# Thirty-two-byte gaps between the activation buffers of an fp32r feed-forward kernel

## The chip, the cores and the metric

The kernel runs on one core of a Trainium2 chip. The metric is the time of one execution on the device in microseconds (us), as the median over runs. TensorE multiplies: it loads a stationary operand of 128 columns (LDWEIGHTS, PEld in the profile) and streams a moving operand of up to 512 columns through it (MATMUL, PE). Both operands lie in the on-chip buffer memory as 128 partitions of consecutive bytes; the result goes to the accumulators. VectorE (DVE), ScalarE (ACT) and GpSimd (POOL) do elementwise work, SyncE (SP) issues the transfers.

## What is computed

Attention over a local window with block summaries, then a feed-forward layer with a squared relu. Cut to what matters:

```python
# q, k, v: (4, 8, 768, 64); x: (3072, 512); w_in: (512, 2048); w_out: (2048, 512)
scores = [scale * q @ k.T within |i - j| < 16, scale * q @ blockmax(k).T + log(32)]
a = softmax(scores)
x = a @ [v, blockmean(v)]          # heads side by side: 3072 rows of 512
h = x @ w_in
g = s * relu(h) ** 2 + b
out = g @ w_out
```

## The kernel before

The 3,072 rows are taken in twelve chunks `c` of 256. For each chunk the attended values `x` (four tiles of 128 features by 256 rows) are made, then sixteen steps `f`, each for 128 of the 2,048 hidden features. Nearly all matmuls of the feed-forward part are done in fp32r, one quick pass, so each operand is split into an upper part (rounded to fp32r) and a lower part (what is left), and a product takes three matmuls: lower weights with upper x, upper weights with lower x, upper with upper.

- `hidden` (L431 to L446) makes `ph`, 128 features by 256 rows. For each of the three terms and each of four pieces `kc`, the stationary operand is a piece of the weights (`wl_in` or `wh`, 128 columns of 512 bytes) and the moving one a piece of `xh` or `xl` (256 columns, 1,024 bytes). That is twelve matmuls a step, at L444.
- `activate` (relu, then square), `scaled` (L460, times s plus b, on POOL) and `split_rows` (L468, on DVE) make `gh` and `gl`, 1,024 bytes a partition each.
- `project` (L476 to L491) accumulates into two tiles `po`. Here the roles are swapped: the stationary operand is half of `gl` or `gh` (128 columns, 512 bytes), the moving one a row of weights (`wh` or `wl_out`, 512 columns, 2,048 bytes). For each of the two halves `t` come gl with wh, gh with wl_out, gh with wh: six matmuls a step, at L488.

The eight steps of chunk 0 that are not in THREE (f below 8) use plain fp32: one tile `g0` in a place of the ring of `gh`, and each matmul is issued as two passes. The other eight steps of chunk 0 read copies `x0h` and `x0l` of the attended values, which lie in slots of the weights.

Order: chunks 0 and 1 follow a list written by hand (FIRST_ORDER). From chunk 2 on, blocks of four steps alternate: 48 matmuls of `hidden` for four steps, then 24 of `project` for the four steps before them, with transposes (`pt`), scores (`ps`) and attended values (`pav`) of the next chunk between the blocks. Each engine runs its instructions in that order, and waits by semaphores for what it reads and for the last reader of a buffer that it overwrites.

Buffers: pools are laid out one after another in each partition in the order in which they are opened, and within a pool the tiles by first use, each rounded up to 32 bytes. `slots` (16 tiles of 4,096 bytes: raw weights, then the pairs `wh` of in and out) starts at byte 4,864, `wring` (33 tiles of 2,048 bytes, `wl_in`, `wl_out` and the plain weights `wf`) at 70,400, `stage` at 137,984, `p2` at 150,272, `p3` (tiles `qk` and `vw`) at 208,832. In `p2`: two `xh` of 4,096 bytes from 171,968; two `r`; eight `gh` of 1,024 from 182,208; two `xl` of 4,096 from 190,400; two `g`; seven `gl` of 1,024 from 200,640. The tile sizes of weights, x and g are multiples of 512.

Of the kernel before, what the change touches and what calls it, by code (L numbers as in the profile page):

```python
# [11 lines left out]
F32 = mybir.dt.float32  # L12
F32R = mybir.dt.float32r
# [6 lines left out]
P = 128  # L20
# [9 lines left out]
T = NSUB * SUB  # L30
# [4 lines left out]
NKC = DM // P  # L35
# [9 lines left out]
def windowed_attention_then_relu2_ffn(ctx, tc, qk, vwin, kt, vt, kq, vrow, wp, out):  # L45
# [6 lines left out]
    wring = ctx.enter_context(tc.tile_pool(name="wring", bufs=2 * NF + 1))  # L52
    stage = ctx.enter_context(tc.tile_pool(name="stage", bufs=4))
    p2 = ctx.enter_context(tc.tile_pool(name="p2", bufs=2))
    p3 = ctx.enter_context(tc.tile_pool(name="p3", bufs=3))
    ps_po = ctx.enter_context(tc.tile_pool(name="ps_po", bufs=2, space=bass.MemoryType.PSUM))
    ps_h = ctx.enter_context(tc.tile_pool(name="ps_h", bufs=2, space=bass.MemoryType.PSUM))
    ps_s = ctx.enter_context(tc.tile_pool(name="ps_s", bufs=2, space=bass.MemoryType.PSUM))
# [50 lines left out]
    def steps(c):  # L109
        return SECOND if c == 1 else tuple(range(NF))  # L110
# [32 lines left out]
    def whole(key):  # L143
        uses[key] += 1
        return w_f[key] if uses[key] < (2 if key[1] in THREE else 3) else w_f.pop(key)
# [80 lines left out]
    def copy(by_dve, out_, in_):  # L226
        if by_dve:
            nc.vector.tensor_copy(out_, in_)
        else:
            nc.scalar.copy(out_, in_)  # L230
# [11 lines left out]
    qk_t, vw_t, ps_of, pr_of, mn_of, sm_of, pt_of, pT_of, o_of, xt, xl = ({} for _ in range(11))  # L242
# [153 lines left out]
    def attended_part(c, p):  # L396
        kcs = slice(p, p + (1 if c < 2 else 2))
        return kcs, o_of[c, p][:, : (kcs.stop - p) * T].rearrange("p (k t) -> p k t", t=T)

    def attended(c, p, other=False):  # L400
        if p == 0:
            xt[c] = p2.tile([P, NKC, T], F32R if c else F32, name="xh", tag="xh")
        kcs, o = attended_part(c, p)
        copy(other, xt[c][:, kcs], o)

# [53 lines left out]

    def scaled(c, f, other=False):  # L460
        if c == 0 and f not in THREE:
            g = p2.tile([P, T], F32, name="g0", tag="gh", bufs=8)
        else:
            g = p2.tile([P, T], F32, name="g")
        gg[c, f] = (g,)
        (nc.vector if other else nc.gpsimd).tensor_scalar(g, r_of.pop((c, f)), s_col, b_col, ALU.mult, ALU.add)  # L466

    def split_rows(c, f):  # L468
        (g,) = gg[c, f]
        gh = p2.tile([P, T], F32R, name="gh", tag="gh", bufs=8)  # L470
        nc.vector.tensor_copy(gh, g)  # L471
        gl = p2.tile([P, T], F32R, name="gl", bufs=7)
        nc.vector.tensor_tensor(gl, g, gh.bitcast(F32), ALU.subtract)  # L473
        gg[c, f] = gh, gl

    def project(c, f):  # L476
        if f == steps(c)[0]:
            for t in range(T // P):
                po[t] = ps_po.tile([P, DM], F32, name="po", tag="po")
        g = gg.pop((c, f))  # L480
        if c == 0 and f not in THREE:
            terms = [(g[0], whole(("out", f)))]
        else:
            gh, gl = g
            terms = [(gl, w_h["out", f]), (gh, w_l["out", f]), (gh, w_h["out", f])]
        for t in range(T // P):
            for n, (a, w) in enumerate(terms):
                nc.tensor.matmul(  # L488
                    po[t], a[:, t * P : (t + 1) * P], w,
                    start=(f == steps(c)[0] and n == 0), stop=(f == steps(c)[-1] and n == len(terms) - 1),  # L490
                )  # L491

    def evict(c, t, other=False):
        o = stage.tile([P, DM], F32, name="o", tag="stage")
        copy(other, o, po[t])
        bi, ci = place(c)
        r0 = bi * S + ci * T + t * P
        nc.sync.dma_start(out[r0 : r0 + P, :], o)
# [37 lines left out]
    def of(fn, s):  # L536
# [5 lines left out]
        "W": keep_warm, "K": k_max, "k": fill_k, "Z": scores_of_maxima, "S": scores, "M": masked, "E": exps,  # L542
        "N": normalize, "T": transposes, "C": turned, "V": values, "U": values_of_means, "R": mean_of_rows,
        "L": load_k, "F": mean_done, "t": fill_v, "X": attended, "y": attended_low, "Xh": first_upper, "Xl": first_lower,
        "Ai": of(scale_weights, "in"), "Ao": of(scale_weights, "out"), "Bi": of(convert_weights, "in"),
        "Bo": of(convert_weights, "out"), "D": lambda f: convert_weights(("in", f), ("out", f)),
        "Y": hidden_part, "H": hidden, "J": activate, "G": scaled, "g": split_rows, "P": project, "O": evict,
        "hi": of(upper_weights, "in"), "ho": of(upper_weights, "out"), "li": of(lower_weights, "in"),
        "lo": of(lower_weights, "out"),
# [22 lines left out]
    for c in range(2, NC):  # L572
        bi, ci = place(c)
        for p in range(NPAIR):
            base, v_at = NF * (c - 1) - 1, (9, 10, 4, 5)[p]
            tr = 8 + 4 * (p // 2)
            lags = (1, 1, 1, 2, (12, 13, 11, 11)[p], tr, tr, 16, 17)
            m, e0, e1, n, fv, tr, tu, va, xa = (base + lag for lag in lags)
            if ci == 0:
                then(base - 12 + p, LOAD, load_k, bi, p)  # L580
                then(base - 7 + p, ATT, k_max, bi, p)
                if p < 2:
                    for third in range(3):
                        then(base + v_at - 5 + third, LOAD, load_v, bi, p, third)
                        then(base + v_at - 1 + third // 2, ATT, v_sum, bi, p, third)
                    then(base + v_at + 1, ATT, v_mean, bi, p)
            then(base - 6, LOAD, load_unit, c, p)
            then(base + v_at, LOAD, load_values, c, p)
            then(base - 2, ATT, fill_k, c, p)
            for j in range(2):  # L590
                then(base, VISIT, scores, c, p, j)
                then(m, NEXT if p < 2 else ATT, masked, c, p, j)
                then((e0, e1)[j], NEXT if p < 2 else ATT, exps, c, p, j)
            then(n, ATT, normalize, c, p)
            then(fv, ATT, fill_v, c, p)
            then(tr, PE_ATT, transposes, c, p)
            then(tu, CHAIN, turned, c, p)
            then(va, VISIT, values, c, p)
            if p % 2 == 0:
                then(xa, ATT, attended, c, p)  # L600
                then(xa, ATT, attended_low, c, p)
# [4 lines left out]
    for i in range(NF, NC * NF):  # L606
        c, j = divmod(i, NF)
        f = steps(c)[j]

        then(i - i % 4, HID, hidden, c, f)  # L610
        for stage_of in (activate, scaled, split_rows):
            then(i, CHAIN, stage_of, c, f)
        then((i + 4) | 3, PROJ, project, c, f)
        if j == NF - 1:
            for t in range(T // P):
                then((i + 4) | 3, EVICT, evict, c, t)
# [60 lines left out]
```

## Time and profile before

| what | us |
|---|---|
| median of 2 runs (631.05 to 631.11) | 631.08 |
| the profiled execution | 630.93 |
| its span, first to last instruction | 629.2 |
| TensorE matmul busy | 616.5 |
| TensorE weight load busy | 550.7 |
| VectorE, ScalarE, GpSimd busy | 328.3, 308.7, 187.7 |

The busy time of PE is a union of spans that overlap, since a matmul starts before the one ahead of it has left the array. So the pace of matmuls is read from start to start, or from a whole block of them in the chain that ended last. PEclk in the profile is the clock that TensorE was granted, in tenths of full speed. In rows of groups the numbers behind the bar are busy us, mean ns of one, idle us of the engine just ahead of them. In rows of waits the numbers are us in total, times, and the longest in us.

### The profile page before, as it was taken

To read this page: it belongs to the slowest core of one execution; us is meant where nothing else is said; L and a number is where in the kernel's file an instruction comes from. 1 tells how busy PE (TensorE), PEld (TensorE's weight loads), DVE (VectorE), ACT (ScalarE), POOL (GpSimd) and SP (SyncE) were. 2 spreads that over 40 slices of the span, in tenths; PEclk is the share of its full clock that TensorE was granted. 3 is DMA by queue.
4 is the path that set the end of the run, shared out by engine and by line. 5 is a ranking of instruction groups with operands and counts; after the bars stand their busy time and mean duration, and the time that the engine had idled before them with its cause. 6 is when DMAs were issued, how large, how long until landed. Compare 5 with 4: busy or idle time off the path is not lost.

```text
span 629.2 us, 14328 instructions
## 1 busy us (share of the span) xinstructions
PE 616.5 (98%) x5330; PEld 550.7 (88%) x5330; DVE 328.3 (52%) x1092; ACT 308.7 (49%) x939; POOL 187.7 (30%) x351
## 2 busy tenths in 40 slices
PE   6999999999999999999999999999999999999997
PEld 5757878989989998999899999998998999899896
DVE  6999899865354246345454335336435324523311
ACT  4999975453463364265245426436345336323321
POOL 3126442211511422322242331341151151232211
PEclk9999999999999999999999999999999999999999
DMA  8999503006205015203502211600710500200000
GB/s 333 413 416 416 222 26 126 17 2 190 79 18 181 1 44 200 74 19 102 165 20 87 94 44 38 236 19 1 218 62 7 181 0 19 85 2 1 34 1 33
DMA packets 26997, 66.45 MB, mean 106 GB/s; under 512 B 3824, under 2 KB 3824, under 8 KB 26928
## 3 DMA queue, kind: packets, MB, share of 16 engines
q1 hardware_dynamic: 26928, 65.54, 29.3%
q8 instruction: 42, 0.69, 0.5%
q14 instruction: 27, 0.22, 0.1%
HBM read 59.09 MB, written 6.29 MB: 104 GB/s over the span
## 4 chain that ended last, share of the span: by engine, by line
PE 87%; DVE 4%; ACT 2%; issue 1%; POOL 1%; DVEq 0%; POOLq 0%; ACTq 0%
PE po L488 40%; PE ph L444 38%; PE pav L394 3%; PE pt L358 3%; PE ps L308 3%; DVE wf_out L141 1%; POOL g L466 1%; DVE wl_in L155 1%; DVE wf_in L141 0%; DVE wf_in L139 0%; ACT r L458 0%; DVE wf_out L139 0%; ACT wraw L125 0%; ACT wraw L126 0%; ACT r L452 0%
## 5 line engine op out<-in xcount | busy, mean ns | idle before, releaser
L466 POOL TENSOR_SCALAR g<-r,sb_col 128x256 f32<-128x256 f32 x189 | 127.1, 673 | 379.2 <-ACT r L458 256.0
L471 DVE CAST gh<-g 128x256 fp32r<-128x256 f32 x184 | 54.9, 298 | 244.0 <-POOL g L466 244.0
L452 ACT ACTIVATE r<-ph 128x256 f32<-128x256 f32 x179 | 67.6, 378 | 206.1 <-PE ph L444 187.0
L488 PE MATMUL po<-wh,gl 128*128 128x512 f32 x368 | 146.3, 397 | 0.0
L488 PE MATMUL po<-wh,gh 128*128 128x512 f32 x368 | 145.0, 394 | 0.0
L488 PE MATMUL po<-wl_out,gh 128*128 128x512 f32 x368 | 144.2, 392 | 0.0
L444 PE MATMUL ph<-xh,wl_in 128*128 128x256 f32 x704 | 109.9, 278 | 0.1
L444 PE MATMUL ph<-xl,wh 128*128 128x256 f32 x704 | 108.8, 276 | 0.0
L444 PE MATMUL ph<-xh,wh 128*128 128x256 f32 x704 | 108.7, 276 | 0.0
L473 DVE TENSOR_TENSOR gl<-g,gh 128x256 fp32r<-128x256 f32 x184 | 85.8, 466 | 33.6 <-PE po L488 16.4
L444 PEld LDWEIGHTS ph<-xh,wl_in 128*128 128x128 f32 x704 | 96.8, 188 | 4.8 <-issue 0.5
L444 PEld LDWEIGHTS ph<-xl,wh 128*128 128x128 f32 x704 | 93.6, 188 | 0.0
L444 PEld LDWEIGHTS ph<-xh,wh 128*128 128x128 f32 x704 | 93.0, 188 | 0.0
L339 ACT ACTIVATE pr<-pr,mn 128x120 f32<-128x120 f32 x176 | 67.0, 382 | 38.6 <-DVE mn L326 38.4
L458 ACT ACTIVATE r<-r 128x256 f32<-128x256 f32 x184 | 77.0, 418 | 15.2 <-DVE r L454 9.7
L488 PEld LDWEIGHTS po<-wh,gl 128*128 128x128 f32 x368 | 69.1, 188 | 14.8 <-issue 1.4
L488 PEld LDWEIGHTS po<-wh,gh 128*128 128x128 f32 x368 | 69.2, 188 | 14.3
L488 PEld LDWEIGHTS po<-wl_out,gh 128*128 128x128 f32 x368 | 69.2, 188 | 13.8
L270 POOL COPY vw<-vsum 24x256 f32<-24x256 f32 x88 | 41.7, 503 | 20.9 <-DMA vsum<-vmean 9.5
L230 ACT COPY o<-po 128x512 f32<-128x512 f32 x24 | 14.0, 589 | 42.3 <-PE po L488 41.3
L339 ACT ACTIVATION_READ_ACCUMULATOR pr<-pr,mn 128x1 f32 x176 | 33.0, 187 | 0.0
L349 DVE TENSOR_TENSOR pr<-pr,rs 128x480 f32<-128x480 f32 x48 | 32.0, 666 | 1.7
(90 smaller groups left out, 565.4 us busy)
## 6 DMA issues: line engine op xcount, KB each, us to landing
wraw<-in_wp_dram SPq DMA_DIRECT2D x32, 512.0 KB
qk<-in_qk_dram SPq DMA_DIRECT2D x44, 369.0 KB
vw<-in_vwin_dram SPq DMA_DIRECT2D x48, 256.0 KB
out_dram<-o SPq DMA_DIRECT2D x24, 256.0 KB
kraw<-in_kt_dram SPq DMA_DIRECT2D x12, 384.0 KB
vraw<-in_vt_dram SPq DMA_DIRECT2D x12, 252.0 KB
kq<-in_kq_dram SPq DMA_DIRECT2D x4, 512.0 KB
vraw<-in_vt_dram SPq DMA_DIRECT2D x6, 264.0 KB
```

The source lines that it names most:

```text
L270: nc.gpsimd.tensor_copy(vw_t[c, p][WIN:KR, e], vsum[bi][WIN : WIN + NB, 2 * p + e, :].unsqueeze(1).to_broadcast([NB, NSUB, D]),)
L308: nc.tensor.matmul(o, qi, kw[r, i, :], start=True, stop=True)
L339: nc.scalar.activation(pr, pr, AF.Exp, bias=mn_of[c, p][:, n : n + 1], scale=-1.0, accum_out=sm_of[c, p][:, n : n + 1])
L349: nc.vector.tensor_tensor(pr, pr, rs.unsqueeze(2).to_broadcast([P, 4, KR]), ALU.mult)
L358: nc.tensor.transpose(pt_of[c, p][:KR, n * P : (n + 1) * P], pr[:, n, :], ident)
L444: nc.tensor.matmul(ph, w[:, kc * P : (kc + 1) * P], x[:, kc], start=(n == 0), stop=(n == len(terms) - 1))
L452: nc.scalar.activation(r, ph, AF.Relu)
L458: nc.scalar.activation(r, r, AF.Square)
L466: (nc.vector if other else nc.gpsimd).tensor_scalar(g, r_of.pop((c, f)), s_col, b_col, ALU.mult, ALU.add)
L471: nc.vector.tensor_copy(gh, g)
L473: nc.vector.tensor_tensor(gl, g, gh.bitcast(F32), ALU.subtract)
L488: nc.tensor.matmul(po[t], a[:, t * P : (t + 1) * P], w, start=(f == steps(c)[0] and n == 0), stop=(f == steps(c)[-1] and n == len(terms) - 1),
```

## The change

The rings of `xh` (two), `gh` (eight) and `gl` (seven) leave the pool `p2`. Each of their buffers becomes a tile of its own in one of three new pools `px`, `pg` and `pl`, opened behind `p2`, and a tile of 32 bytes that nothing uses is put ahead of a buffer where GAP, LGAP or XGAP say so. `apart` hands out the buffers from a list; `project` gives a step's buffers back when it has issued its matmuls.

```diff
+    px, pg, pl = (ctx.enter_context(tc.tile_pool(name=n, bufs=1)) for n in ("px", "pg", "pl"))
+    XGAP, GAP, LGAP = (0, 32), (0,) + (32,) * 7, (0,) + (32,) * 5 + (0,)
+    free, made = {"xh": [0, 1], "gh": list(range(8)), "gl": list(range(7))}, set()
+    places = {}
+
+    def apart(pool, name, shape, dtype, gaps):
+        if free[name]:
+            n = free[name].pop(0)
+        else:
+            n = next(o[name] for o in places.values() if name in o)
+            next(o for o in places.values() if name in o).pop(name)
+        if (name, n) not in made and gaps[n]:
+            pool.tile([P, gaps[n] // 4], F32, name=f"gap_{name}_{n}")
+        made.add((name, n))
+        return n, pool.tile(shape, dtype, name=name, tag=f"{name}{n}", bufs=1)
...
-            xt[c] = p2.tile([P, NKC, T], F32R if c else F32, name="xh", tag="xh")
+            n, xt[c] = apart(px, "xh", [P, NKC, T], F32R if c else F32, XGAP)
+            free["xh"].append(n)
...
-            g = p2.tile([P, T], F32, name="g0", tag="gh", bufs=8)
+            n, g = apart(pg, "gh", [P, T], F32, GAP)
+            places[c, f] = {"gh": n}
...
-        gh = p2.tile([P, T], F32R, name="gh", tag="gh", bufs=8)
+        nh, gh = apart(pg, "gh", [P, T], F32R, GAP)
         nc.vector.tensor_copy(gh, g)
-        gl = p2.tile([P, T], F32R, name="gl", bufs=7)
+        nl, gl = apart(pl, "gl", [P, T], F32R, LGAP)
+        places[c, f] = {"gh": nh, "gl": nl}
...
+        for name, n in places.pop((c, f)).items():
+            free[name].append(n)
```

By the sizes above, `xh` then lies at 185,280 and 189,408, `gh` at 193,504 and on in steps of 1,056 bytes, `gl` at 201,920 and on in steps of 1,056 (the last in one of 1,024), `xl` at 174,016, and `p3` starts 416 bytes later, at 209,248. The weights stay where they are.

## The prediction

> **What bounds the kernel now.** I read the page first: busy times, granted clock, the chain's shares by engine and line, and the costliest groups.
>
> ```profile
> span 629.2 us, 14328 instructions
> ...
> PE 616.5 (98%) x5330; PEld 550.7 (88%) x5330; DVE 328.3 (52%) x1092; ACT 308.7 (49%) x939; POOL 187.7 (30%) x351
> ...
> PEclk9999999999999999999999999999999999999999
> ...
> PE 87%; DVE 4%; ACT 2%; issue 1%; POOL 1%; DVEq 0%; POOLq 0%; ACTq 0%
> ...
> L488 PE MATMUL po<-wh,gl 128*128 128x512 f32 x368 | 146.3, 397 | 0.0
> L488 PE MATMUL po<-wh,gh 128*128 128x512 f32 x368 | 145.0, 394 | 0.0
> L488 PE MATMUL po<-wl_out,gh 128*128 128x512 f32 x368 | 144.2, 392 | 0.0
> ```
>
> TensorE is busy for 98% of the span at full clock, holds 87% of the chain, and has no idle time ahead of these groups. So the end moves only if matmuls follow each other at another pace. The mean durations (392 to 397 ns) overlap, so the pace has to come from start to start. The chain in order of time gives it by whole blocks, start and length in us:
>
> ```profile
> 131.05 5.66 PE ph L444 x48
> ...
> 346.31 0.87 PE pt L358 x8
> ...
> 598.20 5.47 PE ph L444 x48
> 603.67 5.49 PE po L488 x24
> 609.16 5.47 PE ph L444 x48
> 614.63 11.00 PE po L488 x48
> ```
>
> A block of 24 projection matmuls takes 5.49 us, 228.8 ns each; a block of 48 hidden ones 5.47 us, 114.0 ns each; 8 transposes 0.87 us, 108.8 ns each. One early ph block took 5.66 us instead of 5.47. The timeline (start, length in us) shows single starts; a merged row "x4" is left for the next one by four matmuls:
>
> ```profile
> 347.96 0.39 PE L488 MATMUL po<-wl_out,gh 128*128 128x512 f32 x1
> ...
> 350.02 0.39 PE L488 MATMUL po<-wl_out,gh 128*128 128x512 f32 x1
> ```
> ```profile
> 353.46 0.62 PE L444 MATMUL ph<-xh,wh 128*128 128x256 f32 x4
> ...
> 357.54 0.62 PE L444 MATMUL ph<-xh,wh 128*128 128x256 f32 x4
> ```
> ```profile
> 82.43 0.64 PE L444 MATMUL ph<-x0l,wh 128*128 128x256 f32 x4
> ...
> 84.83 0.39 PE L488 MATMUL po<-wh,gl 128*128 128x512 f32 x1
> ```
> ```profile
> 40.41 0.19 PEld L488 LDWEIGHTS po<-wf_out,g 128*128 128x128 f32 x1 [0.24 <-issue]
> ...
> 42.98 0.19 PEld L488 LDWEIGHTS po<-wf_out,g 128*128 128x128 f32 x1 [0.24 <-issue]
> ```
> ```profile
> 28.74 1.27 PEld L427 LDWEIGHTS ph<-xh,wf_in 128*128 128x128 f32 x6
> ```
>
> Po: nine starts in 2.06 us, 228.9 ns. Ph: nine rows of four, 36 starts in 4.08 us, 113.3 ns (the block's 114.0 holds the first few, which are slower). Ph with x0h or x0l as moving operand: five rows of four, 20 starts in 2.40 us, 120.0 ns. Plain fp32 passes, which move 512 columns in 2.57/6 = 428 ns, run at half the fp32r rate. That gives an unhindered pace: 256 plain columns, (1.27 - 0.19)/5 = 216 ns, stand for 512 fp32r ones; the transposes' 128 plain columns, 108.8 ns, stand for 256. Against these estimates every matmul carries an excess: **po 228.9 - 216 = 12.9 ns, ph 113.3 - 108.8 = 4.5, ph with x0 120.0 - 108.8 = 11.2**.
>
> The excess is what the change can move. In the layout of before, all weight tiles (slots from byte 4864, ring from 70400, sizes multiples of 512) start at 256 modulo 512, and all x, gh and gl buffers (from 171968, 182208, 200640) at 448. So the stationary operand lies 192 bytes behind the moving one in po, 320 in ph (the roles are swapped), and 0 in ph with x0, which sits in a weight slot. Three distances, three excesses: 0: 11.2, 192: 12.9, 320: 4.5. That the same ph operands cost 11.2 at distance 0 and 4.5 at 320 is the one sign in this trace that distance matters; the blocks of 5.66 and 5.47 us, at equal distances, show that it isn't all.
>
> **The change part by part.**
>
> *No engine instruction, DMA or wait is added.* The three rings become single places handed out from a list: the front is taken, a place goes to the back when its projection has been issued. Walking the order of before, every g buffer finds a place whose last reader lies exactly as far back as before, so the waits for places should stay:
>
> ```profile
> POOL g L466 <- DVE gh L471: 32.3, 10, 3.8
> ...
> DVE gl L473 <- PE po L488: 16.4, 10, 2.0
> POOL g L466 <- DVE gl L473: 13.9, 8, 3.1
> ```
>
> DVE waits 16.4 us in all for gl's places, and POOL's scaling is queued behind it (13.9 us). What hides them is the block of four steps that TensorE works ahead. I cost this at 0; if one such wait lost its cover, it is 2.0 us (the longest).
>
> *gh's eight buffers* come to 224, 256, ... 448 bytes from the weights modulo 512; *gl's seven* to 448, 480, 0, 32, 64, 96, 96 (they lie behind gh's gaps). No row shows a fp32r matmul at these distances. I read between the three points on straight lines around the circle of 512: from 192 (12.9) to 320 (4.5) by 2.1 ns per 32 bytes, from 320 to 512 (11.2) by 1.1, from 0 to 192 by 0.3. For gh: 10.8, 8.7, 6.6, 4.5, 5.6, 6.7, 7.9, 9.0, mean 7.5. For gl: 9.0, 10.1, 11.2, 11.5, 11.8, 12.05, 12.05, mean 11.1. Gh is loaded 2 x 368 times, gl 368 times:
> gh: (12.9 - 7.5) x 736 = 4.0 us; gl: (12.9 - 11.1) x 368 = 0.7 us. **Sum: 4.7 us less.**
> Bounds: the whole excess, 12.9 x 1104 = 14.2 us, can't be passed; on the other side the ph block at 5.66 against 5.47 us shows 4.0 ns per matmul that a bad state adds, 4.4 us over 1104. I take the interpolation since its three points are rows of this very pair of streams.
>
> *One of two xh buffers* is moved by 32 bytes: half the blocks' xh terms go from 320 to 288, where the line gives 2.1 ns more, for 704 of the 1408 xh matmuls 1.5 us at most. At least it costs 0:
>
> ```profile
> L444 PEld LDWEIGHTS ph<-xh,wh 128*128 128x128 f32 x704 | 93.0, 188 | 0.0
> ```
>
> ph's weight loads, 188 ns each and with no idle time ahead of them, may set the pace of these matmuls, and a slightly longer stream would lie under them. I take 0, since ph in the late blocks always returns to one pace, and keep 1.5 for the range. *xl* stays at 448.
>
> *Everything behind (qk, vw) moves by 416 bytes.* Scores take both operands from one tile, so their distance stays. For vw against pT it changes, but these are plain fp32, and the nearest row, the transposes, runs at 108.8 ns though pr's tiles of 1984 bytes lie at many distances from ident: 0. If not, a few per cent of a visit:
>
> ```profile
> 568.55 2.02 PE pav L394 x64
> ```
>
> 5% of 2.02 us in eleven visits is 1.1 us. The three rests (2.0, 1.5, 1.1) are for the upper end.
>
> Sum against the profiled execution's own 630.93 us (629.2 span and 1.7 around it): 626.2; the median of 631.08 is 0.15 higher, so **626.4 us**.
>
> **The rivals.**
>
> *A, nothing moves.* The excess belongs to something other than the distance: po's 12.9 ns would be a cost of each load or of each start, and x0's 11.2 a state like that of the 5.66 us block, since x0's matmuls also run early. For it: 5.66/48 = 117.9 ns at an unchanged distance is near x0's 120.0. Against: no x0 group of the timeline comes down to 113. Time: 631.1, within 2 us. The Trainium skill, page "TensorE: Matmul & The Clock Gate", section "Part 2: What happens when you issue a matmul", says this side: TensorE has two independent read ports, so that loading the next weights takes no read bandwidth from the running matmul. By that rule the distance can't matter and the time stays; the 12.9 ns of po and the 113.3 against 120.0 of ph speak against it, without settling it.
>
> *B, slower: the stream doesn't settle.* At one fixed distance the pace repeats; with a new distance at each change of buffer it may stay in the dearer state that the block of 5.66 us shows. Place: each po block. Price: (5.66 - 5.47)/48 = 4.0 ns on 1104 matmuls, 4.4 us: 635.5. It decides if the mean po start goes over 228.9 ns, the block of 24 over 5.49 us. Against it: ph has four moving offsets of 1024 bytes and two stationary ones, and settles.
>
> *C, all of the excess goes,* because only the exact repeat at 192 collides: 631.1 - 14.2 = 616.9. Against it: 0 and 192 are both dear, and new distances include 0 to 96.
>
> **How the numbers follow.** The forecast 0.53 (own range 623 to 629), A 0.26, B 0.14, C 0.07. The range reaches from 621, which leaves out most of C (0.06), to 632.5, which takes in A with its 1.5 us and leaves out most of B (0.12): 0.82 inside. Two per cent, about what a measurement of this kernel can tell from no change, is 12.6 us. Faster by more means under 618.5, 11.4 ns of po's 12.9: only the better half of C, 0.04. Slower by more means over 643.7, 11.4 ns added, more than any rest above together: 0.02. Within: 0.94.
>
> **What would show it.** In the profile after: po blocks of 24 in the chain at 5.39 us instead of 5.49 (4.2 ns each, 24 times); ph blocks still 5.47, or up to 5.52 in every other chunk; x0's matmuls unchanged at 120.0, as nothing of them moves; the three waits for places with the same counts. Within a block, starts with gh in the fourth place (320) should follow faster than with gl in the third (0); if all places go at one pace, the interpolation is wrong and A or C holds. I am wrong outright if po's blocks are longer, or if they are shorter and the span isn't.

## The result and the profile after

The changed kernel takes 639.09 us in the median of two runs (638.97 to 639.20), against 631.08 us before: a ratio of 1.0127, 95% interval 1.0083 to 1.0170. That is 8.0 us slower, where 4.7 us faster was forecast, and outside the range. The page of the profile after, in the lines that answer to those shown of before:

```profile
span 637.4 us, 14324 instructions
...
PE 625.6 (98%) x5330; PEld 557.0 (87%) x5330; DVE 329.1 (52%) x1092; ACT 308.8 (48%) x939; POOL 181.8 (29%) x351
...
PEclk9999999999999999999999999999999999999999
...
L506 PE MATMUL po<-wh,gl 128*128 128x512 f32 x368 | 147.9, 402 | 0.0
...
L460 PE MATMUL ph<-xh,wl_in 128*128 128x256 f32 x704 | 111.0, 280 | 0.1
L460 PE MATMUL ph<-xh,wh 128*128 128x256 f32 x704 | 111.0, 280 | 0.0
L460 PE MATMUL ph<-xl,wh 128*128 128x256 f32 x704 | 110.9, 280 | 0.0
```

The span grew by 8.2 us at the same clock, with the same matmuls and still no idle time ahead of them; TensorE's busy time grew by 9.1 us. The loss is pace, not waiting. The chain of the profile after, in order of time (start and length in us), shows where:

```profile
495.05 5.70 PE ph L460 x48
500.75 0.87 PE pt L373 x8
...
525.03 2.02 PE pav L409 x64
...
540.27 5.57 PE po L506 x24
545.84 5.47 PE ph L460 x48
```

Po blocks of 24 take about 5.57 us instead of 5.49. Ph blocks of 48 take 5.70 us in the chunks that use the moved xh buffer (20 of the 40 late blocks) and 5.47, as before, in 17 of the other 20. Transposes and attended values keep their 0.87 and 2.02 us. Summed from each fp32r matmul's start to the next start, leaving out gaps of 260 ns or more, po went from 245.0 to 248.1 us and ph from 253.8 to 259.1: 3.0 and 5.3 us. The waits for buffer places hardly changed (9, 11 and 6 times instead of 10, 10 and 8):

```profile
POOL g L483 <- DVE gh L488: 31.4, 9, 3.8
...
DVE gl L491 <- PE po L506: 17.2, 11, 2.0
POOL g L483 <- DVE gl L491: 10.0, 6, 2.6
```

### The profile page after: what moved, and what is told of

It is laid out like the page before. It is cut to its first block, busy times and chain, and to the rows that moved or that the text cites. A ratio compares the mean times of both kernels' runs of the same rounds, so it can differ in the third digit from the quotient of the medians.

```text
span 637.4 us, 14324 instructions
## 1 busy us (share of the span) xinstructions
PE 625.6 (98%) x5330; PEld 557.0 (87%) x5330; DVE 329.1 (52%) x1092; ACT 308.8 (48%) x939; POOL 181.8 (29%) x351
## 4 chain that ended last, share of the span: by engine, by line
PE 88%; ACT 3%; DVE 3%; issue 1%; POOL 1%; DVEq 0%; POOLq 0%; ACTq 0%
PE po L506 40%; PE ph L460 39%; PE pav L409 3%; PE pt L373 3%; PE ps L323 3%; ACT wraw L140 1%; ACT wraw L141 1%; POOL g L483 1%; DVE wl_in L170 1%; DVE wf_out L156 1%; DVE wf_in L154 0%; DVE wf_out L154 0%; PE ph L443 0%; ACT r L468 0%; DVE wf_in L156 0%
## 5 line engine op out<-in xcount | busy, mean ns | idle before, releaser
L483 POOL TENSOR_SCALAR g<-r,sb_col 128x256 f32<-128x256 f32 x183 | 117.5, 643 | 381.1 <-ACT r L474 264.1
L506 PE MATMUL po<-wh,gl 128*128 128x512 f32 x368 | 147.9, 402 | 0.0
L460 PE MATMUL ph<-xh,wh 128*128 128x256 f32 x704 | 111.0, 280 | 0.0
L460 PE MATMUL ph<-xl,wh 128*128 128x256 f32 x704 | 110.9, 280 | 0.0
L460 PEld LDWEIGHTS ph<-xl,wh 128*128 128x128 f32 x704 | 95.0, 189 | 0.0
L460 PEld LDWEIGHTS ph<-xh,wh 128*128 128x128 f32 x704 | 95.0, 188 | 0.0
L285 POOL COPY vw<-vsum 24x256 f32<-24x256 f32 x88 | 39.6, 478 | 21.0 <-DMA vsum<-vmean 9.0
```

Of the source, the lines that this page charges most:

```text
L285: nc.gpsimd.tensor_copy(vw_t[c, p][WIN:KR, e], vsum[bi][WIN : WIN + NB, 2 * p + e, :].unsqueeze(1).to_broadcast([NB, NSUB, D]),)
L460: nc.tensor.matmul(ph, w[:, kc * P : (kc + 1) * P], x[:, kc], start=(n == 0), stop=(n == len(terms) - 1))
L506: nc.tensor.matmul(po[t], a[:, t * P : (t + 1) * P], w, start=(f == steps(c)[0] and n == 0), stop=(f == steps(c)[-1] and n == len(terms) - 1),
```

## The experiments

"Pace" below is the mean time from start to start inside the 40 late blocks of 24 po matmuls (without the first gap of each, which can hold a change of work) or of 48 ph matmuls, from the trace's start times. A "distance" is, as in the prediction, how far the stationary operand's buffer lies behind the moving one's: 192 in po and 320 in ph before. "Dear" is a ph block whose weights and x lie as before but which runs at 117.7 or 117.8 ns instead of 113.3 to 113.9. Before, 1 of 40 was dear. In the diffs rows of equal gaps are written short.

One limit holds for all runs: the weights never move, and all of them start at a multiple of 256 bytes. So a distance modulo 256 is also the place of g (or x) itself modulo 256, and no run tells the two apart.

**The two halves of the change.** Only the x buffer, with the g buffers back at 192 (the x pool is opened last, so that nothing else moves but what lies behind):

```diff
-    px, pg, pl = (... for n in ("px", "pg", "pl"))
-    XGAP, GAP, LGAP = (0, 32), (0,) + (32,) * 7, (0,) + (32,) * 5 + (0,)
+    pg, pl, px = (... for n in ("pg", "pl", "px"))
+    XGAP, GAP, LGAP = (0, 32), (0,) * 8, (0,) * 7
```

> Only the second xh buffer is moved by 32 bytes (distance 288 instead of 320 to its weights); all g buffers stay at 192. Theory T1 (a fp32r stream settles to a cheap pace only while the distance stays the same from matmul to matmul; here xh at 288 and xl at 320 alternate) and theory T2 (an odd multiple of 32 bytes between the streams is dear in itself) both expect ph blocks of 5.70 us in half the chunks and 5.47 in the others, po blocks back at 5.49, some 636 us. If the x gap has no part in it: 631 us.

Only the g buffers, at the very distances of the change:

```diff
-    XGAP, GAP, LGAP = (0, 32), (0,) + (32,) * 7, (0,) + (32,) * 5 + (0,)
+    XGAP, GAP, LGAP = (0, 0), (32,) * 8, (0,) + (32,) * 5 + (0,)
```

> Only the g buffers are moved, to the very distances of the change (gh 224 to 448, gl 448 to 96); both xh stay at 320. T1 and T2: po blocks of 24 at 5.57 us, ph blocks at 5.47, some 634 us. Together with e1 it should make up the 8.0 us of the change. If ph still has blocks of 5.70 us, the ph loss comes from the pace that a po block hands over, not from xh.

Measured: x alone 636.06 us, ratio 1.0076 (1.0061 to 1.0091), 4.9 us more. The chain of that run has, in neighbouring chunks:

```profile
505.25 5.70 PE ph L460 x48
...
511.82 5.51 PE po L506 x24
...
532.57 5.46 PE ph L460 x48
538.03 5.49 PE po L506 x24
```

G alone 635.01 us, 1.0059 (1.0044 to 1.0074), 3.8 us more: po at 232.2 ns and 8 of 40 ph blocks dear. The halves add up to 8.7 us, close to the 8.0 of the whole. X alone came as expected; g alone came 1 us over, since ph wasn't expected to have dear blocks there. Neither run tells why.

**One distance for all g buffers.** If the loss came from mixing distances, one new distance would cure it.

```diff
-    XGAP, GAP, LGAP = (0, 32), (0,) + (32,) * 7, (0,) + (32,) * 5 + (0,)
+    XGAP, GAP, LGAP = (0, 0), (32,) + (0,) * 7, (0,) * 7
```

> All fifteen g buffers are moved by the same 32 bytes: distance 224 everywhere instead of 192, nothing alternates. T1: the stream settles again, po blocks of 5.49 us or less, 631 us or less. T2 (odd multiple of 32 is dear in itself): po at 5.57 us or more in every block, 634 us or more.

640.49 us, 1.0145 (1.0128 to 1.0162): as slow as the change, with nothing mixed. Theory T1 falls for po. Its chain has po blocks of 5.60 us and ph blocks in either state:

```profile
584.90 5.45 PE ph L460 x48
590.35 5.60 PE po L506 x24
595.95 5.66 PE ph L460 x48
```

The same edit with another first gap (64, 128, 256, then 96, 160, 192, 224 in the place of 32) measures the other distances, each against runs of the kernel before made beside it:

> All g buffers moved by the same 64 bytes: distance 256 in every po matmul. Uniform 224 gave a po pace of 233.4 ns against 229.1 at 192, so repeating alone doesn't make a distance cheap. T2 (odd multiples of 32 are dear): po back at 229 ns, 631 us. T3 (192 is one of few cheap distances, most others cost 232 to 234): po 232 to 234 ns, blocks 5.57 to 5.61 us, 634 to 640 us depending on how many ph blocks stay in their 117.8 ns state.

> All g buffers moved by the same 128 bytes: distance 320 in every po matmul, where the prediction's line put the cheapest place. The prediction's reading (excess 4.5 ns at 320): po 220.5 ns, blocks of 24 at 5.29 us, 622 us. T3: 229 to 234 ns, nothing near 220, 631 us or more.

> All g buffers moved by the same 256 bytes: distance 448 in every po matmul. T3: 229 to 234 ns, 631 us or more. If distances count modulo 256 only (448 then equals 192): po at 229.1 ns with the same three-step pattern as before, ph as before, 631 us.

> All g buffers at 288, which is 32 modulo 256. So far po goes by distance modulo 256: 192 229.1 ns, 224 and 64 233.4, 0 227.7; 448 equals 192. T3 (each distance has its own pace, not on one line): some pace between 227 and 236 ns, and with the three other runs of this series a circle of eight whose mean tells whether the change's 232.1 ns is just the mean of its distances. T4 (mixing distances costs in itself): the mean of the circle lies clearly under 232.1, at 231 or less. Time 631 to 640 us, by the state in which ph settles.

> All g buffers at 352, 96 modulo 256. The same question: T3 227 to 236 ns and a circle whose mean is near 232.1, T4 a mean of 231 or less. By the prediction's line 221.6 ns, which is excluded if 320 with 233.4 stands.

> All g buffers at 384, 128 modulo 256. If the pattern has a period of 128 bytes, it equals 0: 227.7 ns, and all ph blocks at 117.8 ns, 636.7 us. Otherwise T3: a pace of its own, 227 to 236 ns.

> All g buffers at 416, 160 modulo 256. T3: a pace of its own, 227 to 236 ns; with a period of 128 it would equal 32, the run at 288. The mean over the eight distances decides between T3 and T4 as told for the run at 288.

| g at (modulo 256) | po pace, ns | dear ph blocks of 40 | us | ratio to before (95%) |
|---|---|---|---|---|
| 192 (before) | 229.1 | 1 | 631.08 | |
| 448 (192) | 229.0 | 0 | 630.81 | 1.0000 (0.9989 to 1.0011) |
| 224 | 233.4 | 30 | 640.49 | 1.0145 (1.0128 to 1.0162) |
| 256 (0) | 227.7 | 40 | 636.70 | 1.0090 (1.0060 to 1.0119) |
| 288 (32) | 233.1 | 0 | 633.81 | 1.0057 (1.0034 to 1.0080) |
| 320 (64) | 233.4 | 15 | 637.69 | 1.0105 (1.0076 to 1.0135) |
| 352 (96) | 233.9 | 0 | 635.22 | 1.0069 (1.0046 to 1.0092) |
| 384 (128) | 232.3 | 10 | 635.39 | 1.0074 (1.0045 to 1.0103) |
| 416 (160) | 233.3 | 0 | 634.81 | 1.0065 (1.0042 to 1.0088) |

448 repeats 192 in pace, ph blocks and time, so the table counts distances modulo 256; only this pair shows it. A period of 128 is out: 0 and 128 differ by 4.6 ns, 64 and 192 by 4.3. T2 falls as well: 64 and 128 are even multiples of 32 and as dear as the odd ones. T3 holds: 192 and 0 are cheap, the other six lie between 232.3 and 233.9. The change gives gh all eight places of this circle (mean 232.0); gl's seven buffers stand on six of them (mean 232.1). Measured was 232.1 ns. That fits the mean of the places with no cost for mixing, so T4 falls here.

The run at 256 is the odd one: the fastest po, and yet 5.8 us slower than before. Its chain gives both:

```profile
581.42 5.65 PE ph L460 x48
587.07 5.44 PE po L506 x24
```

Po saves (229.1 - 227.7) x 1104 = 1.5 us, ph loses 40 x (5.65 - 5.47) = 7.2 us, with x and weights where they were. Ph reads no g, and yet where g lies decides the state of its blocks.

**X at other distances.** First the second xh buffer by 64 bytes instead of 32 (XGAP = (0, 64), else as the run with x alone), then all of xh and xl by 32, with xl moved into the pool px and the pools in the same order:

> As e1, but the second xh buffer is moved by 64 bytes (distance 256): xh and xl still alternate between two distances, but both are even multiples of 32. T1: as e1, ph blocks of 5.70 us in half the chunks, 636 us. T2: ph blocks 5.47 us everywhere, 631 us.

```diff
-    XGAP, GAP, LGAP = (0, 32), (0,) + (32,) * 7, (0,) + (32,) * 5 + (0,)
+    XGAP, GAP, LGAP = (32, 0), (0,) * 8, (0,) * 7
...
-            xl[c] = p2.tile([P, NKC, T], F32R, name="xl")
+            xl[c] = px.tile([P, NKC, T], F32R, name="xl", bufs=2)
```

> Both xh and both xl buffers moved by 32 bytes: every ph matmul of the fp32r blocks from chunk 1 on has distance 288, nothing alternates within a chunk; g stays at 192. If the dear ph blocks of the change come from xh and xl standing at two distances (T1): all ph blocks back at 5.47 us, 631 us. If 288 is dear in itself (T3): all forty blocks of 48 at 5.70 us, 0.23 x 40 = 9 us more, 640 us.

With 64 bytes: 637.03 us, 1.0092 (1.0077 to 1.0107), the moved chunks at 118.1 to 118.6 ns. T2, which expected 631 us, falls here too. The run is dearer than with 32 bytes because 8 blocks whose own x hadn't moved ran at 117.8 ns: the first two of chunks 4, 6, 8 and 10, each behind a chunk with moved x. There g lay as before, so its place isn't all that sets the state. The second and third block of one such chunk:

```profile
443.64 5.66 PE ph L460 x48
...
455.68 5.46 PE ph L460 x48
```

With all x at 288: 639.74 us, 1.0138 (1.0108 to 1.0167), all forty blocks at 118.3 ns:

```profile
485.09 5.68 PE ph L460 x48
490.77 5.49 PE po L506 x24
```

So 288 is dear in itself, and x beside xl at another distance adds no more than 0.3 to 0.7 ns (118.6 to 119.0 in the change). T1 falls for ph too.

**What hands a ph block its state.** Three layouts with 192 and 0 (as 256 or 512) together:

```diff
-    XGAP, GAP, LGAP = (0, 32), (0,) + (32,) * 7, (0,) + (32,) * 5 + (0,)
+    XGAP, GAP, LGAP = (0, 0), (64,) + (0,) * 7, (0,) * 7               # pools px, pl, pg: gl 192, gh 256
+    XGAP, GAP, LGAP = (0, 0), (0,) * 8, (64,) + (0,) * 6               # gh 192, gl 256
+    XGAP, GAP, LGAP = (0, 0), (64, 0, 0, 0, 0, 192, 0, 64), (0,) * 7   # 0, and 192 for the blocks' last gh
```

> gh stands at 256 (0 modulo 256, the cheapest po distance, 227.7 ns), gl at 192 (229.1 ns). If po goes by the mean of its distances: (2 x 227.7 + 229.1)/3 = 228.2 ns. Theory H1 (the last gh matmuls of a po block, by their distance, set the state in which the ph block behind starts): ph blocks all at 117.8 ns as with 256 everywhere, 637 us. Theory H2 (the pace repeated over the block sets it, gl included): ph at 113.4 to 113.9 ns in most blocks, 630 us.

> The other way round: gh at 192, gl at 256. Mean of distances: (2 x 229.1 + 227.7)/3 = 228.6 ns. H1: ph blocks at 113.3 to 113.9 ns as before, 630.3 us. H2: a mixed lot of ph blocks, 631 to 636 us.

> All at 0 modulo 256 but the two gh buffers that are last in the blocks of four steps, which stand at 192 modulo 256. Mean of distances: 227.9 ns in po. H1: ph at 113.3 to 113.9 ns in nearly all blocks, then 1.2 ns x 1104 = 1.3 us under before, 629.4 us, under both kernels. If the last step alone doesn't set it: ph at 117.8 ns, 637 us.

633.76 us, 1.0048 (1.0031 to 1.0065), 9 dear blocks; 635.27 us, 1.0073 (1.0058 to 1.0088), 16 dear; 637.43 us, 1.0111 (1.0096 to 1.0126), 39 dear. H1 falls with all three, most plainly with the third, where the last gh stood at 192 and ph stayed dear. H2 fits the counts of dear blocks so far, though not the times. The po paces were 231.0, 230.3 and 228.4 ns, where the means of the distances are 228.2, 228.6 and 227.9: here mixing did cost 0.5 to 2.8 ns, so that the change's exact fit to the mean isn't a law.

What goes with the states is the gap at the seam, from the start of the last po matmul to the start of the first ph matmul (the expectation below calls it the po block's last start-to-start gap), counted over the late ph blocks with x at 320, in the kernels before and after and the twelve runs so far that leave x alone (one more block, behind 225 ns, was cheap):

| gap at the seam, ns | ph blocks behind it | dear |
|---|---|---|
| 226 or 227 | 117 | 116 |
| 229 to 232 | 257 | 48 |
| 233 or more | 165 | 7 |

The 8 dear blocks of the run with 64 bytes also stood behind 226 or 227 ns. Inside the po block the gaps don't separate the states: with the last gh at 192 the last of them was 231 or 232 ns, and 39 of 40 ph blocks were dear. Since the seam ends with ph's own first matmul, its length may be a sign of the state as well as its cause.

That was tried on a layout that ends the block at a slow distance and keeps the rest at 0:

```diff
-    XGAP, GAP, LGAP = (0, 32), (0,) + (32,) * 7, (0,) + (32,) * 5 + (0,)
+    XGAP, GAP, LGAP = (0, 0), (64, 0, 0, 0, 0, 32, 0, 224), (0,) * 7   # 0, and 32 for the blocks' last gh
```

> As the run with the last step's gh at 192, but these two buffers stand at 32 modulo 256 (po pace 233 ns when uniform, and ph good after it in all forty blocks); the others at 0. Theory H3 (what counts is the phase at the end of the po block: a block whose last start-to-start gap is 226 or 227 ns hands over the 117.8 ns state, one that ends in 231 ns or more mostly the 113.4 ns state): the blocks end in 231 ns or more, ph at 113.3 to 113.9 ns in most of the forty blocks, po near 229 ns, 630 to 632 us. If the rest of the block decides: ph at 117.8 ns, 637 us.

630.83 us against 630.65 beside it, 1.0002 (0.9993 to 1.0012). The forty seams take 230 or 231 ns (one 235), and all forty ph blocks are cheap. First a pair of the run with the last gh at 192, then one of this run:

```profile
593.89 5.65 PE ph L460 x48
599.55 5.45 PE po L506 x24
```

```profile
587.13 5.47 PE ph L460 x48
592.60 5.48 PE po L506 x24
```

H3's forecast came, and H2 falls, since the rest of the block is the one that left ph dear before. The 6.6 us against the run with 192 come from the places of these two buffers alone: that is shown. That the end of the po block hands the state on is argued from the seams; VectorE writes the same buffers while ph runs, and no run separates that from po's reading. This version equals the kernel before and doesn't beat it; no layout tried does.

## Why the prediction was wrong

**What bounds the kernel: right.** Time moved only through the pace of fp32r matmuls, and the place of the buffers does move it: 32 bytes for all g buffers made the time 1.0145 times as long. Rival A falls. But the excess is not what a place can free: the best po pace, 227.7 ns, is 1.4 ns under before, of the 12.9 that were counted over the estimate of 216. What in the chip ties the pace to the place, no run here shows. The Trainium skill, page "TensorE: Matmul & The Clock Gate", section "Part 2: What happens when you issue a matmul", gives the load of the next weights and the running matmul separate read ports, so that the load takes no read bandwidth from the matmul. Rival A's inference from it, that the distance can't matter, does not agree with the po pace of 229.1 against 233.4 ns at two distances of the same operands; whether bandwidth is shared, no run shows.

**No waits added, and the rests behind (qk, vw): right.** The wait rows stand nearly as before, pt at 0.87 and pav at 2.02 us. The matmuls with x0h or x0l, which nothing moved, kept their 120 ns.

**The interpolation: the step that failed for po.** "I read between the three points on straight lines around the circle of 512." Three things in it were wrong. The circle is 256, as far as 448, which equals 192, shows it. Po and ph don't share a curve: the line took 320 from ph, where it is cheap, and expected 220.5 ns in po, which measured 233.4. Nor do they share one if the distance is counted from the weights to g or x: then 192 is cheap and 224 dear in both, but at 256 po is at its cheapest and ph, with the second xh there, ran at 118.1 to 118.6 ns. And between points there is no line: two cheap places, six dear ones within 1.6 ns. Before stood on one of the cheap two, which the line couldn't know: with one point of po's curve, every new place was read off another kernel stage. In place of 4.2 ns less the change got 3.0 more (232.1 against 229.1): 3.3 us over 1104 matmuls instead of -4.7. That is what the prediction named as being wrong outright: longer po blocks, 5.57 us for the 5.39 expected.

**The moved xh buffer: the step that failed for ph.** "I take 0, since ph in the late blocks always returns to one pace", with 1.5 us as the most. It returned at 320; at 288 the cheap state was never reached, and the half that moved cost 4.9 us in the run with x alone. The row of weight loads with no idle time ahead of them was read as slack for the stream. It held none: about 5 ns more per matmul (118.6 to 119.0 against 113.4 to 113.9) showed in full, and for all three terms of the block, where the 1.5 us were counted for the moved xh alone (for 704 matmuls; the buffer serves six of the eleven chunks, 768). With 5.3 us against po's 3.0 this was the larger loss. The row that warned of it, the early ph block of 5.66 us at 117.9 ns, was on the table; it was priced under rival B for po only.

**Rival B: the sign and nearly the size in po, but not the mechanism.** B put 4.4 us on po blocks above 5.49 us from changing distances; 3.3 us came, at 5.57 us a block. That closeness is luck: the uniform run at 224 has no changing distance and is dearer still. Where mixing did cost, it was with 192 and 0 together, which the change does only among other places. The state that B took from the 5.66 us block is real, and was seen in ph only.

**The range** ended at 632.5 us, with rival A and its 1.5 us inside and most of B, 635.5, outside. Even B fell 3.6 us short. What no term held is that ph could lose its cheap state altogether: 40 blocks at 0.18 to 0.23 us, 7 to 9 us. That stands behind every run above 636 us, in part where only some of the blocks were hit and po was slower too.

## What to carry to other kernels

Where matmuls follow each other without a gap, take the pace from start to start and compare it over buffers before moving any of them: one trace in which all buffers share a distance says nothing of other distances, and a point borrowed from another stage with swapped roles says as little. A few runs, each with all buffers shifted alike, measure the curve. Look at the next stage too, since where one block's buffers lie can set the state of the block behind it, and a block that became faster can cost more than it saves.

## What the runs showed of the hardware

The pace of fp32r po matmuls depends on where g lies modulo 256 bytes, with the weights at multiples of 256: from 227.7 to 233.9 ns over eight places, at the same granted clock (0.999 to 1.000 in the profiled uniform runs). Whether the distance to the weights or the place alone counts isn't shown. Ph at one distance, 320, has two steady paces, with block means of 113.3 to 113.9 and of 117.7 to 117.8 ns and none between, so a block stays in the one it starts with. Behind a seam of 226 or 227 ns it is nearly always the slow one (116 of 117). With x at 288 in all or part of the terms only means of 118.3 to 119.0 ns were seen in the late blocks.
